# Second layer: the first pair's seven-product form from chunk 1 on, its input sums made ahead of chunk 0, the output weight converted wholly in the first layer

## The chip, the cores and the metric

The program runs on one core of a Trainium2 chip. The metric is the device time of one execution in microseconds, as the median of several runs. Five engines work beside each other, each through its own queue in order: TensorE (PE, with its weight loads as PEld), VectorE (DVE), ScalarE (ACT), GpSimd (POOL) and SyncE (SP), which here issues nearly all transfers.

## The reference

```
q_n, k_n = rmsnorm(q, g_q), rmsnorm(k, g_k)            # q, k, v: 4 x 12 x 448 x 64
attn = softmax(q_n @ k_n.T / sqrt(64)) @ v
x = attn.transpose(0, 2, 1, 3).reshape(1792, 768)
h = x @ moe_w_in                                       # 768 x 2048
x = (s * relu(h)**2 + b) @ moe_w_out                   # 2048 x 768
h = x @ moe2_w_in                                      # 768 x 2048
out = (h * cos(h)) @ moe2_w_out                        # 2048 x 768
```

All four weight matrices are stored in 64 bits. The result is in float32, and the kernel keeps that precision.

## The kernel before

Each float32 operand of a large product is held as a high part and the rest (`halves`, `halve`, `low`: ACT makes the high part, DVE or POOL subtracts it), and a product is three matmuls: high times high, low times high, high times low (`products`, L145). The 1792 rows are four batches of 448 tokens; a matmul takes 448 columns as a rule.

The program has three parts. First comes attention, with pieces of the first layer between its steps. Then the first layer goes on in 8 chunks of 256 hidden columns for batches 2 and 3 (segment 3 in `segs`). From chunk 2 of that on, the four block products are made as seven (`unit_seven`, L692). The units `unit_out_1` (L791) multiply a chunk into six output tiles for both batches: 6 matmuls into a PSUM tile `po` (three buffers), which DVE adds to `acc` (L808). In the last chunk each finished `acc` tile goes to DRAM (L812) and is split at once into the second layer's input tile `x_1_b..` (L816 on ACT, L817 on DVE or POOL).

The second layer's first product has 8 chunks too. The batches are two pairs, `pr` 0 (batches 0, 1) and `pr` 1 (batches 2, 3). A chunk of a pair is either four plain units (`plain_in`, 4 x 18 = 72 matmuls) or seven products (`mixed_in`, 7 x 9 = 63 matmuls), as `MIXED` says: from chunk 2 for the first pair, from chunk 3 for the second. Seven products need sums of the inputs, t1 to t4, and of the weights, s1 to s4. `mix_tasks(pr, c)` makes the input sums of one third of the rows: it fetches four tiles `xs` from DRAM (L884), DVE makes four differences one after another (L878), ACT the high parts (L874), POOL and DVE two low parts each (L869). `in_tasks` converts a chunk's weights from 64 bits (`convert`: ACT L552 and L553, POOL L554 or DVE, DVE L555 and L556), makes the sums (L936) and splits them (ACT L942, POOL L943).

`chunk_tasks(ck)` lists what is prepared during chunk `ck` for the chunks behind it; `spread_out` places it between the chunk's units. Chunk 0's first four units stand between the output units of the first layer's last chunk. The first product's results h go through DRAM (`put`, L1007), for 384 columns of pair 0 after h cos(h) is made (L993 to L999).

`out_weight(n)` converts one of the 32 halves of the output weight's 16 row blocks and writes it to DRAM: transfer in (L975), `convert`, transfer out (L979). `OWN` = 20 of them stand in the first layer between `begin` and `after`, where they use the four tiles e0 to e3; the other 12 in the second layer's chunks 1 to 6. `prepare_w` (L1208) reads the blocks back and splits them.

The last part, `second_out`, multiplies h cos(h) by the output weight: 5 groups of token tiles, 16 blocks `f` each. The input of step n is asked for by `ask(n)` (L1161) and split by `halve_g(n)` (L1198). The first three, up to `HI` = 2, are asked for during chunk 7 into tiles of the ring `u_tile` (L982), which also holds the seven products' partial sums u1 to u4; the later ones go into `spare`, made of input tiles that are used up.

Tiles come from pools with a fixed number of buffers per tag. The order on each engine is set by the Tile scheduler from the order of the code and the buffers, with a few orders forced by `behind` and `issue_after`. An engine that has to wait holds back all that stands behind it in its queue, and SP's queue is such a queue for transfers.

Of the kernel before, what the change touches and what calls it, by code (L numbers as in the profile page):

```python
# [10 lines left out]
F32 = mybir.dt.float32  # L11
# [32 lines left out]
def body(ctx, tc, q, k, v, g_q, g_k, w1_in, w1_out, s_in, b_in, w2_in, w2_out, out):  # L44
    nc = tc.nc
    B, H, S, D = q.shape
    E = out.shape[1]
    F = w1_in.shape[1]
    P = 128
# [11 lines left out]
    CW = EH  # L61
# [11 lines left out]
    LEAD = 5  # L73
    FETCH = 0, 8, 20
    STEPS = 5, 8, 11, 14, 17, 20, 24, 25, 26, 27, 28, 28, 29, 30
    MIXED = 2, 3
    GROUPS = (0, 1, 2), (3, 4, 5), (6, 7, 8), (9, 10, 11), (12, 13)
    READY = len(GROUPS[0]) * P
    OWN = 20

    const = ctx.enter_context(tc.tile_pool(name="const", bufs=1))
    dram = ctx.enter_context(tc.tile_pool(name="dram", bufs=1, space=DRAM))
    wp = ctx.enter_context(tc.tile_pool(name="wp", bufs=2))
# [735 lines left out]
    half = NE // 2  # L819
    NAMES_X = [f"b{1 + i}{1 + j}" for i in range(2) for j in range(2)]  # L820
    X = [{}, {}]
    W = {}
# [13 lines left out]
    def slot(where, name):  # L836
        pool, tag, bufs = place(where)
        return pool.tile([P, 2 * S], F32R, tag=tag, name=name, bufs=bufs)
# [5 lines left out]

    PLAIN_A = {"b11": "ah0 al0 ah1", "b21": "al1 ah2 al2", "b12": "bh0 bl0 bh1", "b22": "bl1 bh2 bl2"}
    FIRST = [(name, c) for name in ("b11", "b21", "b12", "b22") for c in range(half)]
    PLAIN_B = "e3 e0 al4 e1 ah5 e2 al5 gh1 gl1 gh2 gl2 gh0".split()
    MIX = [["bh3 bl3 bh4 bl4", "bh5 bl5 ah3 al3", "ah4 bh0 bl0 bh1"], ["gl0 gh gl s0", "s1 s2 s3 s4", "s5 e0 e1 e2"]]

    def f32(z):  # L850
        return z.bitcast(F32)
# [12 lines left out]
    def mix_tasks(pr, c):  # L864
        x, to = {}, {}

        def low(name, eng):
            hi, lo = to[name][:, :S], to[name][:, S:]
            z = eng.tensor_tensor(lo, x[name], f32(hi), ALU.subtract)  # L869
            if eng is nc.vector:  # L870
                behind(z, "DVE")

        def high(name):
            behind(nc.scalar.copy(to[name][:, :S], x[name]), "ACT")  # L874

        def minus(name, y, z):
            w = {"t1": "x11", "t3": "x12", "t2": "x22", "t4": "x21"}[name]
            behind(nc.vector.tensor_tensor(x[w], x[y], x[z], ALU.subtract), "DVE")  # L878
            x[name] = x[w]

        def fetch_all():
            for n, (name, b, cc) in enumerate((("x11", 0, c), ("x12", 1, c), ("x22", 1, c + half), ("x21", 0, c + half))):
                x[name] = wp.tile([P, 2 * CW], F32, tag=("wl", "wh")[n // 3], name=f"xs_{pr}_{c}_{name}", bufs=3)[:, :S]
                nc.sync.dma_start(x[name], stash[1, 2 * pr + b, cc])  # L884
            for name, where in zip(("t1", "t3", "t2", "t4"), MIX[pr][c].split()):
                to[name], _ = x_slot(pr, name, c, where)

        return [fetch_all, lambda: minus("t1", "x12", "x11"), lambda: (high("t1"), minus("t3", "x22", "x12")),
                lambda: (low("t1", nc.gpsimd), high("t3"), minus("t2", "x22", "t1")), lambda: (low("t3", nc.vector), high("t2"), minus("t4", "x21", "t2")),
                lambda: (low("t2", nc.gpsimd), high("t4")), lambda: low("t4", nc.vector)]  # L890
# [68 lines left out]
    def names_of(ck):  # L959
        names = []  # L960
        if ck >= min(MIXED):
            names += ["a11", "s2", "s3", "s1", "a12", "a22", "s4"]
        if ck < max(MIXED):
            names += [z for z in ("a11", "a12", "a21", "a22") if z not in names]
# [124 lines left out]
    def spread_out(lists, steps):  # L1089
        at = []  # L1090
        for n, tasks in enumerate(lists):
            at += [(int((z + 0.5) * steps / len(tasks)), n, z, task) for z, task in enumerate(tasks)]
        return [(z, task) for z, _, _, task in sorted(at, key=lambda v: v[:3])]

    def chunk_tasks(ck):
        lists = [in_tasks(ck + 1, names_of(ck + 1))] if ck < NCK - 1 else []
        for pr in range(2):
            if ck + 1 == MIXED[pr]:
                mixing = [z for c in range(half) for z in mix_tasks(pr, c)]
                lists.append(mixing + [lambda: None] * (len(mixing) // 2))  # L1100
        rest = 2 * NF - OWN
        if ck and ck < NCK - 1:
            each = [OWN + z for z in range(rest) if z * (NCK - 2) // rest == ck - 1]
            if each:
                lists.append([lambda z=z: out_weight(z) for z in each])
        if ck == NCK - 1:
            n = NEARBY
            lists.append([lambda: None] * (n + 2) + [lambda z=z: prepare_w(z) for z in range(n)])
            lists.append([lambda: None] * 12 + [lambda z=z: (ask(z), z < HI and halve_g(z)) for z in range(HI + 1)])
        return lists  # L1110

    def second_in(ck):
        W["xa1"] = True
        steps = []
        for pr in range(2):
            if ck >= MIXED[pr]:
                steps.append(mixed_in(ck, pr))
            else:
                steps.append(map(plain_in, [ck] * 4, (0, 0, 1, 1), (2 * pr, 2 * pr + 1) * 2))
        total = sum(7 if ck >= MIXED[pr] else 4 for pr in range(2))  # L1120
        todo = spread_out(chunk_tasks(ck), total)
# [8 lines left out]
    HI, TIMES, TURNED, RESIDUE, ROUNDED, ASKED = 2, 3, 4, 5, 6, 8  # L1130
# [29 lines left out]
    @staged  # L1160
    def ask(n):  # L1161
        gi, f = STEPS_2[n]
        u = work[n, "g"] = temp(n, "g") if spare else u_tile(f"g2_{n}")[:, :len(GROUPS[gi]) * P]
        at = 0
        for pr, j0, size in columns(gi):
            nc.sync.dma_start(u[:, at:at + size], hd[f, pr][:, j0:j0 + size])
            at += size
# [29 lines left out]
    @staged  # L1197
    def halve_g(n):  # L1198
        u = work.pop((n, "g"))
        size = u.shape[1]  # L1200
        t = part(f"gp_{n}")
        hi, lo = ready[n] = t[:, :size], t[:, CW:CW + size]
        in_line("ACT", nc.scalar.copy(hi, u))  # L1203
        in_line("POOL", nc.gpsimd.tensor_tensor(lo, u, f32(hi), ALU.subtract))  # L1204
# [30 lines left out]
    def second_out():  # L1235
        po = {}
        for n, (gi, f) in enumerate(STEPS_2):
            if f == 0:
                po = {(t, eh): bank(f"po2_{gi}_{t}_{eh}")[:, :EH] for t in GROUPS[gi] for eh in range(2)}
            hi, lo = ready.pop(n)  # L1240
            for z, t in enumerate(GROUPS[gi]):
                cols = slice(z * P, (z + 1) * P)
                for eh in range(2):
                    es = slice(eh * EH, (eh + 1) * EH)
                    for k, (a, m) in enumerate(products([hi[:, cols], lo[:, cols]], [w[:, es] for w in W["out", f]])):
                        mm(po[t, eh], a, m, start=(f == 0 and k == 0), stop=(f == NF - 1 and k == 2))
            if n == 0:
                for z in range(2 * NF, 2 * NF + 9):
                    spare.append(f32(slot(homes[z - 2 * NEARBY], f"sp_{z}")))
            if n:  # L1250
                halve_g(n + HI)
            times_g(n + TIMES)
            turned_g(n + TURNED)
            residue(n + RESIDUE)
            rounded(n + ROUNDED)
            for z in range(HI + 1 if n == 0 else n + ASKED, n + ASKED + 1):
                ask(z)
            if n == 0:
                halve_g(HI)
            if n + NEARBY < NF:  # L1260
                prepare_w(n + NEARBY)
            if f < NF - 1:
                continue
            for t in GROUPS[gi]:
                o = wp.tile([P, E], F32, tag="wh", name=f"o_{t}", bufs=3)
                for eh in range(2):
                    es = slice(eh * EH, (eh + 1) * EH)
                    if eh:
                        in_line("ACT", nc.scalar.copy(o[:, es], po[t, eh]))
                    else:  # L1270
                        in_line("DVE", nc.vector.tensor_copy(o[:, es], po[t, eh]))
                    if t == 2 * NT - 1:
                        store(t, o, es, (nc.sync, nc.scalar)[eh])
                if t < 2 * NT - 1:
                    store(t, o, slice(0, E), nc.sync)
# [13 lines left out]
    early = {}  # L1289
# [106 lines left out]
    prepare = {}  # L1396
# [4 lines left out]
    after = units.index(("seven", 0, 3, NCK - 1, 0, 2))  # L1401
    for z in range(OWN):
        prepare.setdefault(begin + z * (after - begin) // OWN, []).append((out_weight, z))
    for z in range(2 * NE):
        prepare.setdefault(after + 1 + z * 10 // (2 * NE), []).append((load_x, (0, *FIRST[z])))
    for z in range(4):
        prepare.setdefault(after + 1 + 3 * z, []).append((first_part, z))
    entry = units.index(("in1", 1, 4, 0, 0, 0))
    for z, task in spread_out(chunk_tasks(0), len(units) - entry):
        prepare.setdefault(entry + z, []).append((lambda _, task=task: task(), None))  # L1410
    debt = 0.0
# [3 lines left out]
    for n, u in enumerate(units):  # L1415
# [24 lines left out]
        for cost in {"in": unit_in, "in1": unit_in_1, "seven": unit_seven, "out": unit_out}[u[0]](*u[1:]):  # L1440
            debt += cost * rates[min(seg, 1)]
            while debt > 0:
                c = next(steps, None)
# [42 lines left out]
```

## Time and profile before

| | |
|---|---|
| Times of three runs | 1239.08, 1240.49, 1241.17 us (median 1240.49) |
| The profiled execution | 1241.64 us |
| Its span, first to last instruction | 1239.9 us |
| PE busy | 1204.9 us (97%) |
| PEld / DVE / ACT / POOL busy | 1026.3 / 829.9 / 820.6 / 715.9 us |
| Mean granted clock of TensorE | 0.992 |

In the trace, attention and its pieces of the first layer run to about 540 us, the first layer's last segment to 779, the second layer's first product from 746 to 993 (chunk 0 to 793.7, chunk 1 to 823.4, chunk 2 to 852.3), and the output product from 993 to the end. Matmul ends are modelled and overlap, so a stretch of PE is read from start to start.

### The profile page before, as it was taken

Reading aid. Unit: us, or ns where it says so; the run is one execution under the profiler, and the core shown is the slowest. Engines: PE = TensorE matmul, PEld = TensorE weight load, DVE = VectorE, ACT = ScalarE, POOL = GpSimd, SP = SyncE. Lnnn points to the kernel's source line nnn. Section 1 sums busy time; section 2 is a strip of 40 time slices with the busy share of each in tenths; the row PEclk is TensorE's granted clock in tenths of the full one; section 3 lists DMA queues with packets and bytes.
Section 4 is the critical chain, followed back from the end, with each engine's and each line's share of the span. In section 5 each row is a group of like instructions: output and inputs, shape, how many; then the busy total and the mean of one; then the engine's idle time right before and its main releaser. Section 6 shows DMA issues by size and latency. Waiting matters only on the chain.

```text
span 1239.9 us, 19524 instructions
## 1 busy us (share of the span) xinstructions
PE 1204.9 (97%) x6476; PEld 1026.3 (83%) x6476; DVE 829.9 (67%) x1358; ACT 820.6 (66%) x1833; POOL 715.9 (58%) x862
## 2 busy tenths in 40 slices
PE   7999999999999999999999999997999989999998
PEld 5555777777777877889989989986999979999998
DVE  6888779767668674784676768389887734444432
ACT  4788888876666664658666675455555535888775
POOL 4777647464544525546777657376554344767655
PEclk9999999999999999999999999998999989999999
DMA  5334336344433332744443445466545573232321
GB/s 143 93 108 124 103 95 199 113 133 130 126 97 125 97 125 77 254 150 132 145 140 122 128 137 187 135 186 193 185 161 185 178 232 104 76 97 71 92 82 42
DMA packets 123605, 164.35 MB, mean 133 GB/s; under 512 B 15856, under 2 KB 111600, under 8 KB 123504
## 3 DMA queue, kind: packets, MB, share of 16 engines
q1 hardware_dynamic: 123184, 162.87, 42.5%
q8 instruction: 51, 0.84, 0.3%
q14 instruction: 50, 0.41, 0.1%
q10 hardware_dynamic: 320, 0.23, 0.1%
HBM read 115.74 MB, written 47.32 MB: 132 GB/s over the span
## 4 chain that ended last, share of the span: by engine, by line
PE 49%; DVE 4%; DMA 2%; issue 1%; ACT 1%; POOL 1%; SPq 0%; ACTq 0%; DVEq 0%; POOLq 0%
PE po L1021 18%; PE po L800 10%; PE ph_s L1021 5%; PE ph_a L1021 4%; PE ph_s L709 4%; PE ph_a L709 3%; PE ph L1030 2%; PE ph L764 2%; DVE xs_x L878 1%; DMA hd<-u 1%; DMA xs_x<-yd 1%; DVE x_t L869 0%; DMA g<-hd 0%; DVE u L1058 0%; PE ph L1021 0%
## 5 line engine op out<-in xcount | busy, mean ns | idle before, releaser
L1021 PE MATMUL po<-wo_h,gp 128*128 128x384 f32 x896 | 229.6, 337 | 5.7 <-ACT gp L1203 3.7
L1021 PEld LDWEIGHTS po<-wo_h,gp 128*128 128x128 f32 x896 | 163.0, 189 | 6.9 <-ACT gp L1203 4.0
L1021 PE MATMUL po<-wo_l,gp 128*128 128x384 f32 x448 | 150.6, 336 | 0.0
L545 POOL TENSOR_TENSOR wl<-t,wh 128x384 fp32r<-128x384 f32 x94 | 98.5, 1061 | 68.8 <-ACT wh L542 59.1
L808 DVE TENSOR_TENSOR acc<-po,acc 128x448 f32<-128x448 f32 (+2 forms) x168 | 101.4, 616 | 54.0 <-PE po L800 53.3
L1204 POOL TENSOR_TENSOR gp<-sp,gp 128x384 fp32r<-128x384 f32 (+1 forms) x77 | 89.9, 1170 | 75.6 <-ACT gp L1203 73.8
L354 ACT ACTIVATE pr<-sc,top 128x448 f32<-128x448 f32 x161 | 102.3, 640 | 17.3 <-DVE top L342 16.9
L342 DVE TENSOR_REDUCE top<-sc 128x1 f32<-128x448 f32 x168 | 98.1, 614 | 15.5 <-PE sc L327 14.7
L1181 DVE SCALAR_TENSOR_TENSOR sp<-sp,sp 128x384 f32<-128x384 f32 (+1 forms) x64 | 37.4, 584 | 88.0 <-ACT sp L1174 75.0
L379 PE MATMUL tp<-ident,pr 128*112 128x128 f32 x672 | 95.2, 278 | 1.1 <-DVE pT L391 0.5
L379 PEld LDWEIGHTS tp<-ident,pr 128*112 128x112 f32 x672 | 74.7, 134 | 24.9 <-issue 13.3
L800 PE MATMUL po<-gh,wh 128*128 128x448 f32 (+1 forms) x240 | 92.1, 386 | 3.1 <-DVE acc L808 2.5
L764 PE MATMUL ph<-xha,wh 128*128 128x448 f32 (+2 forms) x240 | 89.8, 375 | 0.0
L764 PE MATMUL ph<-xla,wh 128*128 128x448 f32 (+2 forms) x240 | 88.3, 368 | 0.0
L764 PE MATMUL ph<-xha,wl 128*128 128x448 f32 (+2 forms) x240 | 88.2, 367 | 0.0
L800 PE MATMUL po<-gh,wl 128*128 128x448 f32 (+1 forms) x240 | 87.8, 366 | 0.0
L800 PE MATMUL po<-gl,wh 128*128 128x448 f32 (+1 forms) x240 | 87.5, 366 | 0.0
L1021 PEld LDWEIGHTS po<-wo_l,gp 128*128 128x128 f32 x448 | 84.8, 189 | 0.0
L414 PE MATMUL av<-pT,rawv 112*64 112x448 f32 x384 | 80.0, 546 | 0.7 <-PE rt L398 0.7
L542 ACT CAST wh<-t 128x384 fp32r<-128x384 f32 x112 | 53.3, 510 | 34.6 <-PE po L800 19.8
L774 POOL TENSOR_TENSOR gl<-gt,gh 128x448 fp32r<-128x448 f32 (+2 forms) x40 | 48.0, 1202 | 47.3 <-ACT gh L773 44.5
L1021 PE MATMUL ph_s<-x_t,ps 128*128 128x448 f32 x297 | 66.1, 379 | 8.6 <-ACT ps L942 6.6
(229 smaller groups left out, 3278.5 us busy)
## 6 DMA issues: line engine op xcount, KB each, us to landing
raw<-in_moe_w_in_dram SPq DMA_DIRECT2D x64, 384.0 KB, 3.6
rawo<-in_moe_w_out_dram SPq DMA_DIRECT2D x32, 384.0 KB, 3.4
wd<-t SPq DMA_DIRECT2D x64, 192.0 KB, 2.8
raw<-in_moe_w_out_dram SPq DMA_DIRECT2D x32, 384.0 KB, 3.5
hd<-u SPq DMA_DIRECT2D x44, 224.0 KB, 2.5
t<-wd SPq DMA_DIRECT2D x48, 192.0 KB, 2.6
sp<-hd SPq DMA_DIRECT2D x45, 192.0 KB, 2.4
wo<-to SPq DMA_DIRECT2D x32, 192.0 KB, 2.2
```

The lines of the kernel that those rows point to most:

```text
L342: line("DVE", nc.vector.tensor_reduce(top, st[i]["sc", c][j][1][:, :S], axis=AX.X, op=ALU.max, negate=True))
L354: e = line("ACT", nc.scalar.activation(pr, sc[:, :S], AF.Exp, bias=st[i]["top"][:, at], scale=scale, accum_out=st[i]["sums"][:, at]))
L379: mm = [nc.tensor.transpose(tp[:, kc * P:(kc + 1) * P], pr[:, kc * CP:(kc + 1) * CP], ident) for kc in range(NCH)]
L414: mm.append(nc.tensor.matmul(st[i]["pa"][j * D:(j + 1) * D, :], st[i]["v"][:, j, kc, :], st[i]["pT"][:, j, kc, :], start=(kc == 0), stop=( ...
L542: z = nc.scalar.copy(wh, w)
L545: casts.append((count["needed"], z, eng, eng.tensor_tensor(wl, w, wh.bitcast(F32), ALU.subtract)))
L709: z = nc.tensor.matmul(po, a, m, start=(c == 0 and n == 0), stop=(c == half - 1 and n == 2))
L764: nc.tensor.matmul(h, a, m, start=(c == 0 and n == 0), stop=(c == NE - 1 and n == 2))
L800: marks["out"] = nc.tensor.matmul(po, a, m, start=(f == 0 and n == 0), stop=(f == CF - 1 and n == 2))
L808: marks["DVE"] = nc.vector.tensor_tensor(at, po, at, ALU.add)
L1021: z = nc.tensor.matmul(*args, **kw)
L1204: in_line("POOL", nc.gpsimd.tensor_tensor(lo, u, f32(hi), ALU.subtract))
```

## The change

The first pair takes the seven-product form from chunk 1 on. Its input sums for c = 0 and 1 are made around the entry of chunk 0 and fetched into e0 to e3, those for c = 2 in chunk 0. The second pair's sums are spread over chunks 1 and 2. All 32 halves of the output weight are converted in the first layer. The tiles of the last input blocks are exchanged, so that e0 to e3 are taken late, and `ask(2)` is issued in `second_out`, behind step 0, where `spare` exists.

```diff
-    MIXED = 2, 3
+    MIXED = 1, 3
-    OWN = 20
+    OWN = 32
...
-    PLAIN_B = "e3 e0 al4 e1 ah5 e2 al5 gh1 gl1 gh2 gl2 gh0".split()
-    MIX = [["bh3 bl3 bh4 bl4", "bh5 bl5 ah3 al3", "ah4 bh0 bl0 bh1"], ["gl0 gh gl s0", "s1 s2 s3 s4", "s5 e0 e1 e2"]]
+    PLAIN_B = "al4 gh1 ah5 gl1 al5 gh2 gl2 e0 e1 e2 e3 gh0".split()
+    MIX = [["bh3 bl3 bh4 bl4", "bh5 bl5 ah3 al3", "ah4 bh0 bl0 bh1"], ["gl0 gh gl s0", "s1 s2 s3 s4", "s5 gh1 gl1 gh2"]]
...
         def fetch_all():
+            early = [f32(slot(f"e{2 * c + z}", f"xs_{pr}_{c}_{z}")) for z in range(2)] if not pr and c < 2 else []
             for n, (name, b, cc) in enumerate((("x11", 0, c), ("x12", 1, c), ("x22", 1, c + half), ("x21", 0, c + half))):
-                x[name] = wp.tile([P, 2 * CW], F32, tag=("wl", "wh")[n // 3], name=f"xs_{pr}_{c}_{name}", bufs=3)[:, :S]
+                x[name] = early[n // 2][:, n % 2 * S:(n % 2 + 1) * S] if early else wp.tile([P, 2 * CW], F32, tag=("wl", "wh")[n // 3], name=f"xs_{pr}_{c}_{name}", bufs=3)[:, :S]
...
-        for pr in range(2):
-            if ck + 1 == MIXED[pr]:
-                mixing = [z for c in range(half) for z in mix_tasks(pr, c)]
-                lists.append(mixing + [lambda: None] * (len(mixing) // 2))
+        if ck == 0:
+            lists.append([lambda: None] * 8 + mix_tasks(0, 2))
+        elif ck < MIXED[1]:
+            many = MIXED[1] - 1
+            mixing = W.setdefault("mixing", [z for c in range(half) for z in mix_tasks(1, c)])
+            lists.append(mixing[(ck - 1) * len(mixing) // many:ck * len(mixing) // many] + [lambda: None] * 3)
...
-            lists.append([lambda: None] * 12 + [lambda z=z: (ask(z), z < HI and halve_g(z)) for z in range(HI + 1)])
+            lists.append([lambda: None] * 12 + [lambda z=z: (ask(z), z < HI and halve_g(z)) for z in range(HI)])
...
-            for z in range(HI + 1 if n == 0 else n + ASKED, n + ASKED + 1):
+            for z in range(HI if n == 0 else n + ASKED, n + ASKED + 1):
...
+    for z, task in enumerate(mix_tasks(0, 0) + mix_tasks(0, 1)):
+        prepare.setdefault(entry - max(4 - z // 3, 0) + (z >= 9), []).append((lambda _, task=task: task(), None))
```

Lines of the new program from L883 on stand one number higher, and behind `chunk_tasks` three.

DVE at the end of the first layer, around the sums of output tiles 4 and 5 of chunk 6 (`po_6_4`, `po_6_5`) and the first of chunk 7 (`po_7_0`); the last number of a name tells buffers apart. Before:

```order
L808 TENSOR_TENSOR acc_0_4_2_7054<-po_6_4_3_8948,acc_0_4_2_7054 128x384
L808 TENSOR_TENSOR acc_0_5_2_7082<-po_6_5_2_8973,acc_0_5_2_7082 128x512
L555 SCALAR_TENSOR_TENSOR t_3_8964<-c_p_3_8965,t_3_8964 128x384
L556 SCALAR_TENSOR_TENSOR t_3_8964<-c_p_3_8965,t_3_8964 128x384
L808 TENSOR_TENSOR acc_0_5_2_7082<-po_6_5_3_8981,acc_0_5_2_7082 128x384
L808 TENSOR_TENSOR acc_0_0_2_6909<-po_7_0_2_9031,acc_0_0_2_6909 128x448
```

And now:

```order
L808 TENSOR_TENSOR acc_0_4_2_7065<-po_6_4_3_9074,acc_0_4_2_7065 128x384
L878 TENSOR_TENSOR xs_0_0_9099<-xs_0_0_9099 128x448
L878 TENSOR_TENSOR xs_0_0_9099<-xs_0_1_9100,xs_0_0_9099 128x448
L808 TENSOR_TENSOR acc_0_5_2_7092<-po_6_5_2_9112,acc_0_5_2_7092 128x512
L878 TENSOR_TENSOR xs_0_1_9100<-xs_0_1_9100,xs_0_0_9099 128x448
L555 SCALAR_TENSOR_TENSOR t_3_9090<-c_p_3_9091,t_3_9090 128x384
L869 TENSOR_TENSOR x_0_t_0_9106<-xs_0_0_9099,x_0_t_0_9106 128x448
L808 TENSOR_TENSOR acc_0_5_2_7092<-po_6_5_3_9128,acc_0_5_2_7092 128x384
L878 TENSOR_TENSOR xs_1_0_9137<-xs_1_0_9137 128x448
L878 TENSOR_TENSOR xs_0_1_9100<-xs_0_1_9100 128x448
L556 SCALAR_TENSOR_TENSOR t_3_9090<-c_p_3_9091,t_3_9090 128x384
L878 TENSOR_TENSOR xs_1_0_9137<-xs_1_1_9138,xs_1_0_9137 128x448
```

The differences of the input tiles and a low part of t1 have moved between the sums. From the sum of `po_6_4_3` to that of `po_7_5_3` there stood 33 instructions, and now 49: nine of L878, four of L869 and three of L936 (L937 now) more.

SP at the start of the output product. `g_1` and `g_2` are the inputs of steps 1 and 2 in the ring, `sp` tiles of `spare`, `tw` blocks of the output weight, `hd<-u` results of chunk 7 written out. Before, up to the transfer of step 2's input:

```order
L1007 DMA hd_0_11276<-u_7_0_11214 128x448
L1166 DMA sp_11488<-hd_0_9898 128x384
L1166 DMA sp_11488<-hd_0_9870 128x384
L1007 DMA hd_0_11263<-u_7_0_11238 128x448
L1215 DMA tw_11534<-wo_8337 128x768
L1007 DMA hd_1_11381<-u_7_1_11368 128x448
L1166 DMA sp_11487<-hd_0_9529 128x384
L1166 DMA sp_11489<-hd_0_10198 128x384
L1166 DMA sp_11489<-hd_0_10174 128x384
L1007 DMA hd_1_11406<-u_7_1_11320 128x448
L1166 DMA sp_11487<-hd_0_10752 128x384
L1166 DMA g_2_11460<-hd_0_9420 128x384
```

And now, where step 2's input is the first of the two into `sp_11498`:

```order
L1008 DMA hd_0_11289<-u_7_0_11239 128x448
L1218 DMA tw_11518<-wo_7770 128x768
L1169 DMA g_1_11468<-hd_0_9356 128x384
L1169 DMA sp_11497<-hd_0_10540 128x384
L1169 DMA sp_11497<-hd_0_10527 128x384
L1169 DMA sp_11498<-hd_0_9729 128x384
L1169 DMA sp_11498<-hd_0_9707 128x384
L1008 DMA hd_0_11289<-u_7_0_11227 128x448
L1218 DMA tw_11546<-wo_7982 128x768
```

Step 2's input has moved ahead of five results that are written out, into a tile of `spare`, and one block of the weight has moved ahead of `g_1`.

## Rows read from the trace of the kernel before

**Rows 1.** Waits of PE over the span: total, times, longest

```profile
PE ph_s L1021 <- ACT ps L942: 6.6, 1, 6.6
...
PE po L1021 <- ACT gp L1203: 3.7, 1, 3.7
...
PE po L1021 <- DVE u L1058: 1.6, 1, 1.6
```

**Rows 2.** Timeline of PE, chunks 2 and 3: start, busy, line, tiles, count, wait

```profile
823.44 2.02 PE L1021 MATMUL ph_a<-x_b,pa 128*128 128x448 f32 x9
...
837.66 14.75 PE L1021 MATMUL ph<-x_b,pa 128*128 128x448 f32 x72
852.25 1.99 PE L1021 MATMUL ph_a<-x_b,pa 128*128 128x448 f32 x9
860.84 0.74 PE L1021 MATMUL ph_s<-x_t,ps 128*128 128x448 f32 x1 [6.59 <-ACT ps L942]
862.55 7.74 PE L1021 MATMUL ph_s<-x_t,ps 128*128 128x448 f32 x26 [0.98 <-POOL ps L943]
```

**Rows 3.** Chain that ended last: chunk 3's second pair, chunk 4's first

```profile
875.87 1.86 PE ph_a L1021 x9
...
888.89 1.86 PE ph_a L1021 x9
```

**Rows 4.** Timeline of PE at steps 1 and 2 of the output product

```profile
1000.90 0.34 PE L1021 MATMUL po<-wo_l,gp 128*128 128x384 f32 x1
1004.95 0.69 PE L1021 MATMUL po<-wo_h,gp 128*128 128x384 f32 x1 [3.72 <-ACT gp L1203]
...
1010.67 0.51 PE L1021 MATMUL po<-wo_h,gp 128*128 128x384 f32 x2
```

**Rows 5.** Windows: busy PE, PEld, DVE, ACT, POOL (instructions), PEclk, DMA share, GB/s

```profile
750.18:779.00 28.82, 28.82 (x142) 26.25 (x141) 23.66 (x35) 18.90 (x37) 20.21 (x20) 1.00 0.60 193
818.08:858.89 40.81, 35.09 (x171) 31.57 (x169) 36.01 (x49) 23.34 (x48) 26.71 (x24) 0.98 0.62 196
1006.00:1010.00 4.00, 3.97 (x12) 3.97 (x13) 2.44 (x2) 1.20 (x3) 3.21 (x2) 0.50 0.48 142
```

**Rows 6.** Chain that ended last, the input of step 2

```profile
991.39 4.06 DMA hd<-u
...
996.23 2.95 DMA hd<-u
...
999.24 5.05 DMA g<-hd
```

**Rows 7.** Timeline of DVE, the weight sums s2 of chunks 2 and 3

```profile
818.08 0.55 DVE L936 TENSOR_TENSOR s<-s,pl 128x384 f32<-128x384 f32 x1
...
858.89 1.34 DVE L936 TENSOR_TENSOR s<-s,pl 128x384 f32<-128x384 f32 x1
```

**Rows 8.** Tile view of xs_x, the differences: ns min/median/max, first and last start

```profile
L878 DVE TENSOR_TENSOR xs_x<-xs_x,xs_x x24: 607/790/1576, 779.5 to 865.5; 128x448 f32<-128x448 f32 x24
```

**Rows 9.** Groups on DVE, 794 to 866: busy us, mean ns | idle before

```profile
L878 DVE TENSOR_TENSOR xs_x<-xs_x,xs_x 128x448 f32<-128x448 f32 x21 | 21.7, 1033 | 19.0 <-DMA xs_x<-yd 19.0
```

**Rows 10.** Timeline of DVE: the sum of po_7_0_2

```profile
756.27 0.62 DVE L808 TENSOR_TENSOR acc<-po,acc 128x448 f32<-128x448 f32 x1 [1.76 <-PE po L800]
```

**Rows 11.** Chain that ended last: PE takes that bank again for po_7_1_3

```profile
760.98 2.48 PE po L800 x12
```

**Rows 12.** Waits of SP, 560 to 736: total, times, longest

```profile
SPq L979 <- DVE to L556: 51.2, 16, 7.7
SPq L975 <- ACT to L553: 30.4, 14, 3.1
SPq L570 <- POOL wl L545: 13.7, 11, 2.9
SPq L570 <- POOL wsl L611: 11.5, 8, 2.9
```

**Rows 13.** Windows of the first layer's last segment, columns as in rows 5

```profile
580.00:736.00 156.00, 156.00 (x765) 140.80 (x764) 104.72 (x157) 101.66 (x207) 104.62 (x105) 1.00 0.43 131
```

## The prediction

> **What bounds the kernel now.** I read the page's first table (PE busy 97%), then the waits of PE over the span, PE's timeline and the chain of waits where those waits lie, then windows and DVE, ACT, POOL and SP around each. PE sets the time: 1204.9 us of 1239.9 are matmuls, and all its waits are short. So an edit is worth what it takes from PE's queue, the waits it removes there, and the time after a wait in which PE runs at a lower granted clock. The largest wait [rows 1] is 6.6 us for ACT's split of a weight sum `s`, in chunk 3. A second, 3.7 us for `gp`, stands at step 2 of the output product. At full clock PE issues a 448-column matmul each 0.2067 us: 63 of them lie between 875.87 and 888.89 [rows 3], 13.02 us. The other engines count only where PE waits for them.
>
> **The gains.** (a) Chunk 1 of the first pair falls from 72 matmuls to 63: 9 x 0.2067 = 1.86 us.
>
> (b) Chunk 3's first pair starts at 852.25 [rows 2] and ends at 875.87 [rows 3], 23.62 us for 63 matmuls, 10.60 over the 13.02. Of that 6.59 is the wait for ACT's high part of s2 and 0.98 one for POOL [rows 2]; the rest is pace, for instance 26 matmuls in 7.74 us (0.298 each) behind the wait [rows 2]. ACT isn't late by itself: DVE makes s2 only at 858.89 [rows 7]. From chunk 2's s2 at 818.08 to there DVE is busy 36.01 of 40.81 us with 49 instructions [rows 5], while PE would need 63 + 72 matmuls, 27.9 us, for a chunk. Now 18 of these instructions are gone (eight differences, four low parts, six of conversions for the output weight): 31 x 0.83 (40.81 / 49) = 26 us. The s2 of chunk 1, which is new, has 42 instructions to the next, 35 us, but is made before chunk 1 starts, some 10 us ahead of need. So DVE keeps pace and I take all 10.60. If the fetches of `xs`, for which DVE waited 19.0 us over chunks 1 to 3 [rows 9], hold it up again, some comes back (a rival below).
>
> (c) Chunk 2's first pair takes 837.66 - 823.44 = 14.22 [rows 2], 1.20 over 13.02; the same relief gives that.
>
> (d) Step 2 of the output product. The last matmul of step 1 starts at 1000.90 and the next should follow at 1001.07 (384/448 of 0.2067 is 0.177). It came at 1004.95 [rows 4], and twelve of its matmuls took the 4 us from 1006 to 1010 at a granted clock of 0.50, the 1.2 GHz level [rows 5]; the 17th started at 1010.67 [rows 4]. Undisturbed, 16 x 0.177 = 2.8 us on, it would start at 1003.9: 6.8 lost. The cause is in the chain [rows 6]: `g_2` waits for two results written out from the ring (`hd<-u`, 4.06 and 2.95 us, from 991.39 and 996.23) and then takes 5.05 us itself, from 999.24 to 1004.3. Now it goes into `spare`, and SP issues it ahead of five results. I take 6.8. PE's 1.6 us for `u` [rows 1] stays.
>
> Gains: 1.86 + 10.60 + 1.20 + 6.8 = 20.5 us.
>
> **The costs.** (E) The boundary of the layers. Sixteen more DVE instructions stand between the sum of `po_6_4_3` and that of `po_7_5_3`. The sums free PSUM banks for PE, and each finished `acc` feeds the second layer. From 750.18 to 779.00 DVE is busy 23.66 of 28.82 us [rows 5], so 5.2 us of room. A difference took 0.607 to 1.576 us [rows 8], 1.033 on average while chunks 1 to 3 ran [rows 9]. I take that mean for all sixteen, since POOL is as busy here (20.21 of 28.82 us [rows 5]) as there: 16.5 us, so DVE ends 16.5 - 5.2 = 11.3 late. How much of a lag PE stands is seen at one bank: DVE has added `po_7_0_2` at 756.27 + 0.62 = 756.89 [rows 10], and PE takes the bank again at 760.98 [rows 11], 4.1 us of slack. PE is held up 11.3 - 4.1 = 7.2 us. With 0.607 each it is 9.7 - 5.2 - 4.1 = 0.4; with 1.576, 25.2 - 5.2 - 4.1 = 15.9. A wait of this size may bring the lower level of the clock, as in rows 5: 0 to 3 us more (chunk 3 lost 10.60 - 6.59 - 0.98 = 3.0 that way), I take 1. A sum that stands behind a difference in DVE's queue also waits for that difference's `xs` transfer.
>
> The differences read both operands from SBUF, and the Trainium skill (page "SBUF — State Buffer", section "Who interferes with whom") says that the only contention is on a port pair shared by VectorE and GpSimd, held as an exclusive lock. The spread of rows 8 agrees with that; by the rule the price follows POOL's load at that moment, and more POOL work there would move it to the 1.576 end, which is a rival of its own below.
>
> (F) Twelve more halves of the output weight in the first layer. SP hands over all of that layer's transfers in order. From 560 to 736 it waited 51.2 us for DVE and 30.4 for ACT on account of the 20 conversions there [rows 12], 4.1 us for each; twelve more make 49. With its other two waits, 13.7 and 11.5 [rows 12], that is 106.8 + 49 = 156 of 176 us: it just fits. DVE, ACT and POOL are each busy about 105 of 156 us [rows 13], and the twelve add some 20 to DVE; PE waits for nothing there (156.00 of 156.00 [rows 13]). At the longest wait for one, 7.7 us [rows 12], it would be 106.8 + 92 = 199, 23 us over. I take 1 us, between 0 and 23, near the mean's end since 16 waits show it.
>
> (G) At step 1 a block `tw` now goes ahead of `g_1` on SP, and more is asked for at the start of `second_out`. No row prices it; a `g` transfer that is late costs at most what g_2's did, and a wait without cause costs 0. I take 1 (0 to 2, about the wait for `u` of rows 1 at most, the smallest that PE shows there).
>
> **Sum.** -20.5 + 7.2 + 1 + 1 + 1 = -10.3. The profiled execution took 1241.64 us, 1.15 over the median of the three; 1241.64 - 10.3 = 1231.3, so 1230.2 as a median.
>
> **The rivals.** R1, DVE takes the sixteen instructions at the price of an undisturbed one, 0.607, and the lag is absorbed: E 0.4 and no clock loss, 1240.5 - 20.5 + 0.4 + 2 = 1222.4, and 1220.4 without F and G. For it: 5.2 us of room, and PE has three buffers. Against: rows 9's mean.
>
> R2, the shared port: every one of the sixteen at 1.576, E 15.9, clock 3, F and G 2: 1240.5 + 0.4 = 1240.9, no change. For it: the long ones of rows 8 stand where POOL works. Against: the same row holds as many short ones, and the mean is what it is.
>
> R3, slower: SP in the first layer. If each of the twelve holds SP as the longest did, its fetches of weights fall behind, PE waits 23 us in the segment: 1240.5 - 20.5 + 9.2 + 23 = 1252.2. It decides from some 14 us of overrun on (11.3 eat up the gain). For it: 156 of 176 is nearly full, and four tiles e0 to e3 are all it has. Against: rows 12's mean.
>
> R4, the wait in chunk 3 stays in part, since DVE waits for `xs` transfers in chunk 2 as it did before [rows 9], or the second pair's differences crowd s2 again: b gives 3 in place of 10.60, 1237.8.
>
> **How the numbers follow.** Chances: the forecast (1225 to 1235) 0.46, R1 0.22, R2 0.12, R3 0.10, R4 0.10. The range 1219 to 1240.5 holds the forecast, nearly all of R1, R4 and half of R2, 0.82. About 0.2%, 2.5 us, is what a measurement of this kernel tells from no change. Faster than 1238.0: 0.46 + 0.22, half of R4 and a sixth of R2, 0.75. Slower than 1243.0: nearly all of R3, a quarter of R2, 0.12. The same: 0.13.
>
> **What would show it.** In the profile after: PE's wait for ps in chunk 3 is gone and that first pair takes about 13.0 us; step 2 follows step 1 without a wait, with the clock at 1.00; from 750 to 795 PE waits for `acc` on DVE, some 7 us in all, and L878 there has a mean near 1.0; SP's two waits on account of the output weight from 560 to 736 add up to some 131 us (81.6 + 49), and PE still waits for nothing there. The forecast is wrong if PE waits in the first layer's segment (R3), if the waits for `acc` stay under 2 us (R1) or pass 14 (R2), or if one for a weight sum over 3 us is left in chunks 1 to 3 (R4).

## The result

| | before | changed |
|---|---|---|
| Median of five runs | 1241.17 us (1239.08 to 1242.18) | 1231.35 us (1225.56 to 1234.11) |
| Ratio, 95% interval | | 0.9914 (0.9884 to 0.9943) |
| The profiled execution | 1241.64 us | 1234.11 us |
| Its span | 1239.9 us | 1232.3 us |
| PE busy | 1204.9 us | 1200.3 us |

The kernel became faster by 9.8 us, against 10.3 forecast; the interval goes from 7 to 14 us. The profiled execution is the longest of its five and shows 7.5 us. The sum came out; the terms did not all do so.

Waits of PE over the span of the changed kernel (total, times, longest) answer to [rows 1]:

```profile
PE po L800 <- DVE acc L808: 11.7, 9, 5.1
...
PE ph L1031 <- ACT x_b L816: 1.9, 1, 1.9
```

The waits for `ps`, `gp` and `u` are gone. In their place PE waits for DVE's sums between the layers, as forecast, but most of it in one wait of 5.1 us, which the forecast does not have.

PE's timeline from chunk 1 on (start, busy, line, tiles, count), beside [rows 2, 3]:

```profile
811.87 1.99 PE L1022 MATMUL ph_a<-x_b,pa 128*128 128x448 f32 x9
...
824.64 14.75 PE L1022 MATMUL ph<-x_b,pa 128*128 128x448 f32 x72
839.23 1.99 PE L1022 MATMUL ph_a<-x_b,pa 128*128 128x448 f32 x9
...
866.59 1.99 PE L1022 MATMUL ph_a<-x_b,pa 128*128 128x448 f32 x9
...
879.36 1.99 PE L1022 MATMUL ph_a<-x_b,pa 128*128 128x448 f32 x9
...
892.13 1.98 PE L1022 MATMUL ph_a<-x_b,pa 128*128 128x448 f32 x9
```

Chunk 3's first pair lasts from 866.59 to 879.36, 12.77 us in place of 23.62. But chunk 1 begins only at 811.87, where it began at 823.44 - 144 x 0.2067 = 793.7 before: 18.2 us have been lost by there, and chunks 1 to 3 bring back 15.0, since chunk 4 begins at 892.13 and not at 888.89.

PE's timeline at the boundary of the layers shows where:

```profile
748.77 0.69 PE L800 MATMUL po<-gh_s,wh 128*128 128x384 f32 x1 [5.09 <-DVE acc L808]
...
773.35 0.47 PE L800 MATMUL po<-gh_s,wh 128*128 128x448 f32 x1 [0.87 <-DVE acc L808]
...
789.49 0.47 PE L800 MATMUL po<-gh_s,wh 128*128 128x448 f32 x1 [0.31 <-DVE acc L808]
792.54 0.47 PE L800 MATMUL po<-gh_s,wh 128*128 128x448 f32 x1 [1.16 <-DVE acc L808]
...
796.27 2.70 PE L1031 MATMUL ph<-x_b,p 128*128 128x448 f32 x12 [0.42 <-DVE x_b L817]
800.88 11.15 PE L1031 MATMUL ph<-x_b,p 128*128 128x448 f32 x46 [1.91 <-ACT x_b L816]
```

These waits are 9.8 us. Behind the idle 5.09 us PE ran at the 1.2 GHz level (a granted clock of 0.50) to about 754, so that the window of 748 to 755 has 0.57 (columns as in [rows 5]):

```profile
748.00:755.00 7.00, 6.23 (x20) 5.61 (x21) 6.66 (x10) 6.95 (x15) 6.50 (x6) 0.57 0.73 218
```

The wait of 5.09 us comes before the first added subtraction (760.61 on DVE). The chain that ended last, from 729 on, tells whose it is:

```profile
729.87 3.07 DMA wo<-to
732.95 0.32 SPq L885
...
733.84 3.94 DMA wo<-to
737.84 0.32 SPq L885
...
738.69 4.19 DMA xr_b<-yd
742.90 0.57 ACT x_b L859
```

ACT's timeline has the wait at that point:

```profile
742.90 0.57 ACT L859 CAST x_b<-xr_b 128x448 fp32r<-128x448 f32 x1 [6.97 <-DMA xr_b<-yd]
```

SP holds the transfers `xs` (L885) until the output weight's last halves have left the tiles e2 and e3. Nine transfers `xr_b` (L858) stand behind them in its queue. ACT waits 6.97 us for the first of them, DVE 5.67 us for ACT, and two sums that PE needs stand behind DVE's `x_b`:

```profile
740.21 0.55 DVE L808 TENSOR_TENSOR acc<-po,acc 128x384 f32<-128x384 f32 x1
746.43 1.22 DVE L860 TENSOR_TENSOR x_b<-xr_b,x_b 128x448 fp32r<-128x448 f32 x1 [5.67 <-ACT x_b L859]
...
748.04 1.14 DVE L808 TENSOR_TENSOR acc<-po,acc 128x512 f32<-128x512 f32 x2
```

SP's waits from 560 to 736, against [rows 12]:

```profile
SPq L976 <- ACT to L553: 49.0, 25, 5.6
SPq L980 <- DVE to L556: 34.1, 18, 4.9
```

They are 83.1 us for 32 halves, where 81.6 us had gone on 20 and 131 were forecast. PE was busy 174.66 of the 176 us there, so it stood still for 1.3.

### The profile page after: what moved, and what is told of

It is laid out like the page before. It is cut to its first block, busy times and chain, and to the rows that moved or that the text cites. A ratio compares the mean times of both kernels' runs of the same rounds, so it can differ in the third digit from the quotient of the medians.

```text
span 1232.3 us, 19490 instructions
## 1 busy us (share of the span) xinstructions
PE 1200.3 (97%) x6467; PEld 1025.1 (83%) x6467; DVE 822.7 (67%) x1369; ACT 821.4 (67%) x1834; POOL 717.9 (58%) x866
```

## The experiments

The theory after the result (B): the cost at the boundary is two things, DVE's added subtractions, as forecast, and SP's order, `xs` behind the output weight's writes and ahead of `xr_b`, which was not. The rival (A): all of it is DVE's. On the gains it was open which part of the change had brought each. Each kernel was timed beside the kernel before; the first four of the table shared a chip, the next four a second one, the last four a third.

| run | median us | ratio (95%) |
|---|---|---|
| xs_late | 1227.42 | 0.9884 (0.9870 to 0.9898) |
| no_diff | 1225.38 | 0.9874 (0.9860 to 0.9888) |
| own20 | 1233.74 | 0.9941 (0.9929 to 0.9953) |
| ask_only | 1237.67 | 0.9970 (0.9959 to 0.9980) |
| own32_only | 1233.68 | 0.9942 (0.9921 to 0.9963) |
| ask_back | 1228.96 | 0.9912 (0.9893 to 0.9932) |
| out_early | 1227.13 | 0.9894 (0.9875 to 0.9913) |
| out_mix_early | 1228.71 | 0.9913 (0.9891 to 0.9935) |
| after_again | 1232.75 | 0.9931 (0.9909 to 0.9952) |
| xs_late_again | 1227.55 | 0.9889 (0.9870 to 0.9908) |
| out_early_alone | 1232.31 | 0.9919 (0.9895 to 0.9942) |
| no_diff_late | 1219.88 | 0.9830 (0.9810 to 0.9851) |

### xs_late, and again beside the changed kernel

```diff
-                nc.sync.dma_start(x[name], stash[1, 2 * pr + b, cc])
+                z = nc.sync.dma_start(x[name], stash[1, 2 * pr + b, cc])
+                if early and c:
+                    issue_after(z, marks["xr"])
```

`marks["xr"]` is the latest transfer of `load_x`.

> The changed kernel, with one difference: the four transfers xs of c = 1 for the first pair are issued behind the last of the xr_b transfers on SP, where before they stood ahead of eight of them. In the changed kernel's profile PE waits 5.1 us for DVE at 748.77, and the chain leads from there over DVE's and ACT's x_b to an xr_b transfer that SP issued at 738.69, behind two xs transfers that had waited for the output weight's last write. Theory A (DVE's sixteen added instructions hold up the sums, as the prediction's term E has it): the wait stays, and the time is that of the changed kernel, 1231 us. Theory B (the transfer queue): the 5.1 us and some 2.5 us at the lower clock behind it go, PE's waits for acc between 740 and 752 stay under 1 us together, and the time is some 7 us less, 1224. The small waits from 770 to 800 (4.7 us) stay under both.

> The changed kernel unaltered, on the same chip as the next three, to compare with: 1231 (1225 to 1234, as its five runs had). If the 5.1 us wait at the boundary of the layers belongs to the order of the queue and not to one execution, the profile has it again, 3 to 6 us long.

> The kernel whose xs transfers of c = 1 stand behind the last xr_b, unaltered: 1227 (1225 to 1230). By the queue theory it is 4 us or more below the changed kernel of this call, and has no wait over 1 us between 735 and 755. If the earlier distance between the two was only the pace of the executions, they lie within 1 us of each other.

The first run of xs_late, 1227.42, lies between the 1231 of A and the 1224 of B: the 5.1 us wait went, but one of 2.14 us came at 765.17, where the changed kernel waits 0.87. Timed side by side, the changed kernel took 1232.75 and the new order 1227.55: 5.2 us less (the first measurements of the two, on different chips, say 3.9). The waits of PE at the boundary, in the repeated changed kernel:

```profile
744.49 0.56 PE L800 MATMUL po<-gh_s,wh 128*128 128x384 f32 x1 [4.24 <-DVE acc L808]
768.69 0.47 PE L800 MATMUL po<-gh_s,wh 128*128 128x448 f32 x1 [1.45 <-DVE acc L808]
```

and in the repeated kernel with the new order, where the first one is that at 766.78:

```profile
766.78 0.47 PE L800 MATMUL po<-gh_s,wh 128*128 128x448 f32 x1 [2.15 <-DVE acc L808]
785.98 0.47 PE L800 MATMUL po<-gh_s,wh 128*128 128x448 f32 x1 [0.67 <-DVE acc L808]
```

So the long wait belongs to the order of the queue, which settles B for this part: it recurs with the old order and is gone with the new one. From the last matmul of L709 to the start of chunk 1 PE took 73.7 and 71.0 us with the old order, 68.0 and 67.3 with the new one, so 3.0 to 6.4 us lie where the theory puts them. The two profiled executions of the repetition differ by only 0.5 us (1227.98, the fastest of its six, and 1227.50), since the old order's was 3.2 us ahead at that last matmul (734.77 against 737.98): the medians give the price, the profiles the place.

### no_diff and no_diff_late: without the eight subtractions

```diff
-            behind(nc.vector.tensor_tensor(x[w], x[y], x[z], ALU.subtract), "DVE")
+            if pr or c == 2:
+                behind(nc.vector.tensor_tensor(x[w], x[y], x[z], ALU.subtract), "DVE")
```

`no_diff` is the changed kernel with this, `no_diff_late` is xs_late with this.

> The changed kernel without the eight subtractions of the first pair's input sums for c = 0 and 1 (L878 on DVE, between the layers); the sums then hold one input each. Theory A: PE's waits at the boundary fall to what they were before the change, 2.5 us in all, with the lower clock behind them, so the time falls by some 12 us from 1231 to 1219. Theory B: the 5.1 us wait at 748.77 stays, since the first of these subtractions stands behind it at 760.61; only the small waits from 770 to 800 go (4.7 us, and up to 1.7 us at the lower clock behind them): 1225.

> The kernel whose xs transfers of c = 1 stand behind xr_b, without the eight subtractions of the first pair's input sums for c = 0 and 1 (the sums then hold one input each). What DVE's added work costs alone: by the prediction's term E 7.2 us and 1 us of clock, 1227 - 8 = 1219; by the waits that the profile with them shows from 760 to 800 (2.1, 0.7, 0.4 and 1.9 us, and two stretches of 3.4 us at the lower clock, 1.7 us each) 8.5 us at most. If the splits on ACT hold up the second layer's first chunk and not DVE's subtractions, the 1.9 us wait for ACT stays and the time is 1223 or more.

`no_diff` took 1225.4, the number that B gave, but not for B's reason. The wait at 748 was gone although SP issued `xr_b` late, at 736.90: without the subtractions the scheduler had put two more sums ahead of the `x_b` that waits (DVE's `x_b` waits 3.45 us there, at 745.29), and PE waited 3.21 us for ACT's `p` instead. It tells the two theories apart badly. `no_diff_late` is the clean one: beside xs_late_again it is 7.7 us shorter, and PE's waits between 700 and 810 are two for `x_b` on ACT (total, times, longest):

```profile
PE ph L1034 <- ACT x_b L816: 1.2, 2, 1.1
```

The 7.7 us are the price of eight subtractions; the other eight of the sixteen added instructions, four low parts and three weight sums among them, are still in.

### out_early, out_early_alone and out_mix_early

```diff
-        prepare.setdefault(begin + z * (after - begin) // OWN, []).append((out_weight, z))
+        prepare.setdefault(begin + z * (after - 6 - begin) // OWN, []).append((out_weight, z))
```

`out_early` is xs_late with this, `out_early_alone` the changed kernel with this. `out_mix_early` is `out_early` with one edit more:

```diff
-        prepare.setdefault(entry - max(4 - z // 3, 0) + (z >= 9), []).append((lambda _, task=task: task(), None))
+        prepare.setdefault(entry - 8 + z // 2, []).append((lambda _, task=task: task(), None))
```

> The changed kernel with xs of c = 1 behind xr_b, and also the 32 conversions of the output weight spread over a stretch that ends six units earlier. By the queue theory the last writes are then done before xs and xr_b are asked for, so nothing waits there; the kernel with xs of c = 1 behind xr_b took 1227.4, and this one gains at most its 0.2 us wait at 744 more, unless the tighter stretch makes SP late in the first layer (term F): 1227, or up to 1232 if PE then waits between 560 and 736.

> The changed kernel with one number altered: the conversions of the output weight end six units earlier; xs stays ahead of xr_b on SP. If it is the late write of the output weight that holds SP (xs waits for its tile), the wait at the boundary goes as it did with xs behind xr_b: 1227. If it is xs standing ahead of xr_b that costs the time, whatever it waits for, the wait stays: 1231.

> As the kernel whose conversions of the output weight end six units earlier, and also the first pair's input sums for c = 0 and 1 start four units earlier, two tasks in a unit, so that DVE's eight differences stand from output tile 2 of chunk 6 on. By term E (DVE's added instructions hold up the sums and the split inputs at 765 to 800: waits of 2.1, 0.7, 0.4 and 1.9 us in the kernel with xs of c = 1 behind xr_b) these waits fall to 1 us or less, and with the lower clock behind them some 5 us are won: 1222. The rival: DVE's order, with xr_b's low parts and differences between the sums of chunk 6, makes PE wait earlier, from 735 to 755, by as much: 1227 to 1230.

`out_early` was as expected, 1227.1. `out_early_alone` won nothing (1232.3): SP still issued its last two `xs` only at 734.66, held by the output weight's write, and eight `xr_b` from 743.00 on, so ending the conversions six units earlier did not take the late write out of their way. The long wait was gone all the same: PE's longest between the layers were 1.91, 1.27 and 1.16 us, and from the last matmul of L709 to chunk 1 it took 68.2 us, as in xs_late. But with the same conversions in a shorter stretch PE waited for `acc` 0.66, 1.68, 0.66 and 1.16 us at 618, 641, 670 and 698, 4.2 us, where the changed kernel has 1.2 in all, and from the first to the last matmul of L709 it took 174.1 us (171.9 and 170.2 in the changed kernel). So in that profile the time stayed though the wait did not: the gain behind was paid for in front. Whether that is all that the median kept isn't shown. `out_mix_early` is a miss, 1228.7: with the subtractions among the sums of chunk 6, PE waits for `acc` nine times from 741 to 789, 1.46 us at most. The rival of its expectation held: the waits moved.

### ask_only and ask_back: step 2's input

`ask_only` is the kernel before with the two lines of `chunk_tasks` and `second_out` that move `ask(2)`; `ask_back` is the changed kernel without them:

```diff
-            lists.append([lambda: None] * 12 + [lambda z=z: (ask(z), z < HI and halve_g(z)) for z in range(HI)])
+            lists.append([lambda: None] * 12 + [lambda z=z: (ask(z), z < HI and halve_g(z)) for z in range(HI + 1)])
...
-            for z in range(HI if n == 0 else n + ASKED, n + ASKED + 1):
+            for z in range(HI + 1 if n == 0 else n + ASKED, n + ASKED + 1):
```

> The kernel before with one part of the change: ask(2) is issued in second_out behind step 0, into spare, and not in chunk 7 into the ring. By the prediction's term d the wait of 3.7 us for gp at step 2 and the stretch at clock 0.50 behind it go, 6.8 us: 1234. The rival is that the wait for u at the start of the output product (1.6 us) goes too, as it has in the changed kernel, since a tile of the ring is free for it: 8.4 us or more, 1232. If g_2's lateness has another cause than the ring, the time stays within 2.5 us of 1241.

> The changed kernel with one part undone: ask(2) stands again in chunk 7 and its tile in the ring. By the prediction's term d the wait for gp at step 2 comes back with the stretch at the lower clock, 3.7 us and 6.8 us in all: 1231 + 7 = 1238. The rival: with the conversions gone from chunk 6 the results hd are written earlier, so the ring's tile comes free earlier, g_2 is in time anyway, and the time stays within 2.5 us of 1231.

`ask_only` won 3.3 us, not 6.8. The wait for `gp` went, but the one for `u`, which its rival saw go too, grew from 1.64 to 4.14 us:

```profile
997.58 0.94 PE L1021 MATMUL po<-wo_h,gp 128*128 128x384 f32 x2 [4.14 <-DVE u L1058]
```

`ask_back` lost nothing (0.9912 against 0.9914), and has no wait at all in the output product's first steps. So in the changed kernel the place of `ask(2)` is worth nothing that could be measured.

### own20 and own32_only: the output weight's conversions

One number each: `OWN` is 20 in the changed kernel, and 32 in the kernel before.

> The changed kernel with OWN = 20 again: twelve of the output weight's conversions go back into chunks 1 to 6, all else as changed. Theory A: the waits at the boundary stay as in the changed kernel (7.4 us from 735 to 800 for acc), and nothing is won. Theory B: SP has no late write of the output weight ahead of xs and xr_b, so the 5.1 us wait goes and the boundary costs 2 to 5 us in waits. On chunks 1 to 3: if the six conversions were what made s2 late in chunk 3, a wait for ps of 2 us or more comes back there; if the spreading of the second pair's sums alone did it, none does. The time: 1231 to 1237 by A, 1222 to 1229 by B.

> The kernel before with one part of the change: OWN = 32, so that all halves of the output weight are converted in the first layer; the sums of inputs are made where they were. The prediction's term F has this cost 1 us (0 to 23) in the first layer's waits of SP. The prediction's term b would have part of chunk 3's wait go with six of the eighteen instructions: 6.6 us falls to some 2 us. What the changed kernel showed adds that the wait for u before the output product (1.6 us, 4.1 us in the run with ask(2) alone) goes, since SP and DVE have no conversion left in chunk 6. Forecast: 1241 - 4.5 (with the pace behind that wait) - 1.6 + 1 = 1236. If the late writes of the output weight alone bring the 5.1 us wait at the boundary of the layers, without the early transfers xs, it is 1242 or more.

`own20` has no long wait at 748, as B said. Its waits between the layers are still 6.5 us, more than B's 2 to 5, with one of 3.23:

```profile
765.84 0.47 PE L800 MATMUL po<-gh_s,wh 128*128 128x448 f32 x1 [3.23 <-DVE acc L808]
```

It took 1233.7, in the range of A and not of B, since PE also waits at the start of the output product:

```profile
993.10 1.01 PE L1022 MATMUL po<-wo_h,gp 128*128 128x384 f32 x2 [3.56 <-DVE u L1059]
994.88 1.01 PE L1022 MATMUL po<-wo_h,gp 128*128 128x384 f32 x2 [0.46 <-DVE u L1059]
```

DVE waits there 4.34 us for a result `hd<-u` to land. In chunk 3 there is only a wait of 0.35 us, though the conversions are back; it is the only one for `ps` (total, times, longest):

```profile
PE ph_s L1022 <- POOL ps L944: 0.3, 1, 0.3
```

`own32_only` won 7.0 us, 2 more than forecast, but not by the forecast's terms: 4.5 us were to come from chunk 3, whose first pair still took 22.1 us (23.62 before). It shows the opposite of `own20`: no wait for `u`, but those of chunk 3 are there, and a shorter one for `gp`:

```profile
861.04 0.47 PE L1021 MATMUL ph_s<-x_t,ps 128*128 128x448 f32 x1 [1.55 <-ACT ps L942]
867.11 7.17 PE L1021 MATMUL ph_s<-x_t,ps 128*128 128x448 f32 x26 [5.61 <-POOL ps L943]
1002.61 0.44 PE L1021 MATMUL po<-wo_h,gp 128*128 128x384 f32 x1 [1.66 <-ACT gp L1203]
```

So chunk 3's wait does not hang on the conversions. The rest of the change takes it away, in which the spread sums of inputs are what relieves DVE there; no run has the spreading by itself. Taking the conversions out of the chunks takes away the wait for `u` and about half of that for `gp`. Of the 7.0 us some 4.3 lie there by the profile (from chunk 4 to the 16th matmul of step 2, 4.5 us go on waits and the lower clock, and 8.8 did before); where the others lie isn't shown, since the profiled execution, 1239.41, is the longest of its seven.

## Why the prediction was right in its sum, point by point

**(a) to (c): right.** Chunks 2 and 3 lasted from 823.44 to 888.89 before, 65.45 us, and last from 839.23 to 892.13 now, 52.90. That is 12.55 less against 11.80 for b and c; 0.75 is the pace of the matmuls (below). The part of b's reasoning that counted the conversions among the relief was not needed: `own20` has them back and waits 0.35 us, and without them alone (`own32_only`) the wait stays.

**(d): the gain came, its cause was wrong.** From the start of chunk 4 to the 16th matmul of step 2 (the prediction counts the one at 1010.67 as the 17th, so its 6.8 should read 6.9), PE took 1010.67 - 888.89 = 121.78 us before and 1003.14 - 892.13 = 111.01 now: 10.8 less. Of this 2.0 is pace: xs_late, with no wait there either, took 113.0 at the slower one. The other 8.8 are the 6.9 and about 1.9 for `u`. The failed step is "`g_2` waits for two results written out from the ring", with the tile and SP's order as the remedy, and that PE's 1.6 us for `u` "stays". The results themselves were late, and the conversions in the chunks made them so: without the conversions `u` is in time and `gp` less late (1.66 us in `own32_only`), and in the changed kernel `g_2` is in time wherever it is asked for (`ask_back`). With the conversions, moving `ask(2)` takes away the wait for `gp` but lets the one for `u` grow (`ask_only`), and half of the 6.8 us is lost again. By what way twelve conversions delay `hd` by some 4 us (the queue of SP, the DMA engines or DVE) was not tried.

**(E): right in its size, not in its parts.** Forecast were 7.2 us of waits and 1 of clock for sixteen instructions. `no_diff_late` measures 7.7 for the eight subtractions; by E's own sum the other eight alone would fit into room and slack (8.3 against 5.2 + 4.1 us), so the two agree. But PE waits 5.2 us from 760 to 800 with the subtractions (xs_late_again) and 1.2 without, and with them two stretches of 3.4 us, behind waits of 2.15 and 1.90 us, run at the 1.2 GHz level (a granted clock of 0.50), without them none. So some 4 us are waits and up to 3.4 the clock. In the changed kernel PE's waits for `acc` from 750 to 795, forecast as some 7 us, are 2.3. The subtractions took 1.09 and 1.08 us there on average from 755 to 777, near the 1.033 of [rows 9]:

```profile
L878 DVE TENSOR_TENSOR xs<-xs,xs 128x448 f32<-128x448 f32 x4 | 4.4, 1090 | 0.0
...
L878 DVE TENSOR_TENSOR xs<-xs 128x448 f32<-128x448 f32 x4 | 4.2, 1079 | 0.0
```

POOL was busy 19.88 of those 22 us (columns as in [rows 5]):

```profile
755.00:777.00 22.00, 21.13 (x101) 18.36 (x100) 21.33 (x25) 10.55 (x23) 19.88 (x17) 1.00 0.27 79
```

So the rival by which a busy POOL takes all of them to 1.576 us did not come about. The Trainium skill (page "SBUF — State Buffer", section "Who interferes with whom") lets DVE and POOL contend for one port pair under an exclusive lock. The spread in this trace, 0.61 to 1.58 us for one kind of subtraction, agrees with that, but with POOL busy nine tenths of the time the mean was hardly above that of [rows 9].

**(F): the working was off, and a wait was missed.** A half holds SP for 2.6 us (83.1 over 32), not 4.1. Of the 23 us that were possible PE waited 1.2 before 736; from the first to the last matmul of L709 it took 171.9 us against 169.3 before (170.2 in the repeated run), so F is 0.9 to 2.5 against 1. What it brings is a gain: 7.0 us in `own32_only`, alone. In the changed kernel it is worth only 1.0 to 2.4 us, by the medians of `own20` and the two measurements of the changed kernel, since it also costs at its end: the last writes hold `xs`, and `xs` holds `xr_b`. The prediction looked at which DVE instructions are added at the boundary and not at the transfers that were put ahead of others on SP there: 5.2 us.

**(G)**: no wait at step 1, so 0 and not 1.

**The sum.** In the profiled execution a matmul of `po_6` that started at 735.63 before starts 2.8 us later, at 738.41, and the stretch from there to chunk 1 takes 15.4 us more, where 8.2 were forecast. Waits of 9.8 us and 10.2 us at half the clock (stretches of 6.8 and 3.4 us, at most 5.1 us lost) explain up to 14.9 of it. Chunk 1 then gains 2.4, chunks 2 and 3 12.55, the rest 10.8: 18.2 - 25.7 = -7.5. Costs of 10.2 and gains of 20.5 were forecast: both were too small. What was left out on one side, SP's order above all, has nothing to do with what was left out on the other, the wait for `u` and some 3.3 us of pace, which the program does not set. That they came near to cancelling is luck.

**A better version.** xs_late, the changed kernel with four transfers behind `xr_b`, took 1227.4 and 1227.6, 0.9884 and 0.9889 of the kernel before. The subtractions still cost it 7.7 us, and the one attempt to place them better failed.

## What to carry to other kernels

When a step is moved to an earlier place, list its transfers in the issuing queue too, see what each waits for there, and what stands behind it: a transfer that waits for a tile delays all that follow, and the engine that shows the wait may be three steps away. A wait that the chain puts down to a late transfer can have its cause in what delayed the data before it; undoing the suspected line in the changed kernel as well as doing it alone in the old one tells the two apart.

## What the runs showed of the hardware

At a granted clock of 1.00, 448-column matmuls run at one of two paces, 0.2067 or 0.2027 us each, for long stretches. The windows from 880 to 980 hold matmuls of the same kind in the kernel before, in the changed kernel and in xs_late (columns as in [rows 5]); the counts of PE differ by 9:

```profile
880.00:980.00 100.00, 100.00 (x486) 90.81 (x485) 83.37 (x130) 51.65 (x107) 51.55 (x55) 1.00 0.53 179
```

```profile
880.00:980.00 100.00, 100.00 (x495) 92.67 (x494) 67.84 (x114) 46.33 (x92) 43.37 (x47) 1.00 0.39 134
```

```profile
880.00:980.00 100.00, 100.00 (x486) 90.83 (x485) 65.10 (x112) 46.86 (x91) 40.34 (x45) 1.00 0.42 140
```

The first run of xs_late kept the slower pace to the end of the product, and the repeated one the faster: one pair lasts 13.02 us there (872.61 to 885.63) and 12.77 here (872.79 to 885.56). So it is not the program that sets it. From chunk 1 on, in all these runs, the pace changes only where PE was interrupted: at a wait, at a stretch at the lower clock, and once (`own32_only`, at 833.2) where two matmuls came 0.14 us late. Why one pace or the other follows is not known. Over the 925 such matmuls from 800 to 990 the two differ by 3.7 us, which is much of the spread within one kernel's runs, and reason to compare several runs where a few microseconds matter.
